# One element of the last output piece is copied by ScalarE and VectorE and multiplied by TensorE ahead of the program's final branch

## The chip, the cores and the metric

The kernel runs on one core of a Trainium2 chip. A core has five engines with instruction streams of their own: TensorE (PE; its weight loads are listed as PEld), VectorE (DVE), ScalarE (ACT), GpSimd (POOL) and SyncE (SP), which here issues the DMAs. The metric is the device time of one execution in microseconds (us); lower is better. Names that end in q in the profile (PEldq, ACTq, DVEq, SPq) stand for an engine's sequencer: the part that reads the stream, waits on semaphores, branches and issues DMAs.

## The reference, cut to what matters

```python
for t in range(S):                      # S = 768, per batch (4) and head (8), D = 48
    cur = u * k[t] ⊗ v[t]
    y[t] = r[t] @ (state + cur)
    state = w * state + k[t] ⊗ v[t]
x = y rearranged to [3072 tokens, 384]
h = x @ w_in                            # 384 x 2048
g = 0.5 * h * (1 + erf(h / sqrt(2)))
out = g @ w_out                         # 2048 x 384
```

A decaying recurrence over 768 positions comes first, then a two-layer perceptron on its 3072 rows of 384 numbers.

## The kernel before, in words

The recurrence is cut into 6 chunks of 128 positions and computed with matrix products, in 24 groups (6 chunks by 4 pairs of heads). The perceptron runs behind it, chunk by chunk: 512 rows at a time, the 2048 hidden features in 16 blocks of 128, which makes 96 steps. A step has nine products that make the hidden block (`product1`, L697, into `Hp`), a GELU on ScalarE (L729, L730), a difference on VectorE (L731) and nine products that add to the three output banks (`product2`, L741, into `O0`, `O1`, `O2`).

The order of all work is set ahead of time by the class `Plan`. Every piece of work is given to it by `add(engine, ns, due, function, r=names read, w=names written)`, or by `dma(...)` for SyncE. `Plan.run` then plays the list through with estimated times and lets each engine take the piece with the earliest due time among those that could start; the functions are called in that order, and this is the order of each engine's stream. The waits between engines are put in by the framework from the tiles that are read and written.

The last step is written out in `moe2`. Its output is cut into four pieces: two of 512 columns from banks O0 and O1, and two of 256 columns from O2 and Y. ScalarE (L780) and VectorE (L777) in turn multiply a bank by 256 into an SBUF tile (`raw0`, `raw1`, `raw2`, and for the last piece `Nb`, called `N[NP]` in the code), and SyncE stores each piece with a DMA of its own (L783). The last piece is made by VectorE.

Behind the planned work stands `with tc.If(plain[0] < LP * NP)` (L918). It holds a general version of the kernel, for decay rates that lie outside a range that is tested on the chip. Every engine compares the count that it loaded at L807 and branches. With these inputs the condition is false, and each engine jumps over the general version to the program's end (L1004), where a barrier gathers all five engines: SyncE first waits there for all DMAs to land. The general version is long on TensorE and ScalarE, short on the others.

Of the kernel before, what the change touches and what calls it, by code (L numbers as in the profile page):

```python
# [9 lines left out]
F32 = mybir.dt.float32  # L10
# [46 lines left out]
class Plan:  # L57
# [16 lines left out]
    def add(self, eng, ns, at, fn, r=(), w=(), port=False):  # L74
        n = len(self.ops)
        deps = set()
        for x in r:
            deps.add(self.writer.get(x))
            self.readers.setdefault(x, []).append(n)
        for x in w:  # L80
            deps.add(self.writer.get(x))
            deps.update(self.readers.pop(x, ()))
            self.writer[x] = n
        deps -= {None, n}
        self.ops.append((eng, ns, at, fn, deps, port or eng == "pool"))
        self.reads.append(set(r))
        self.writes.append(set(w))
        return n

    def dma(self, nbytes, at, fn, r=(), w=()):  # L90
        self.add("sp", nbytes, at, fn, r, w)
# [99 lines left out]
def rwkv_gelu_mlp(tc, rkT, rkv, wuT, uN, wmlp, r, k, vT, w, u, out):  # L191
    nc = tc.nc
    with ExitStack() as ctx:
        cst = ctx.enter_context(tc.tile_pool(name="cst", bufs=1))
# [6 lines left out]
        def sb(shape, dt, name, pool=None):  # L201
            return (pool or wk).tile(shape, dt, name=name)

        AA = psp.tile([128, 2, 512], F32, name="A")
        A = [AA[:, i] for i in range(2)]
# [47 lines left out]
        add, dma = plan.add, plan.dma  # L253
        dve = lambda n: 65 + n / 0.96
        dve2 = lambda n: 65 + n / 1.92
        act = lambda n: 60 + n / 1.2
# [30 lines left out]
        for dst, src, x in ((diag2, diag, "diag"), (past2, past, "past")):  # L287
            for h in range(2):
                add("act", 245, LATER, lambda dst=dst, src=src, h=h: nc.scalar.copy(
                    out=dst[64 * h:64 * h + 64], in_=src[64 * h:64 * h + 64, 64 - 64 * h:128 - 64 * h]),  # L290
                    r=[x], w=[f"{x}2{h}"])
# [21 lines left out]
        for x in wa:  # L313
            add("act", act(2 * DM), LATER, lambda x=x: nc.scalar.copy(
                out=x.bitcast(F32).rearrange("p (a n) -> p a n", a=2),
                in_=zeros[:, 0:DM].bitcast(F32).unsqueeze(1).to_broadcast([128, 2, DM])), r=["zeros"], w=["wa"])
# [223 lines left out]
        U0 = NB * HALF  # L540
        SLOTS = NP + 1
        done = sb([1, 1], F32, "done", cst)

        quarter = lambda x: slice(64 * x, 64 * x + D)
        heads = lambda x: slice(D * x, D * x + D)
# [154 lines left out]
        def hidden(m):  # L700

            i, k_ = NCH % 2, NSTEP - 1 - m
            if k_ == 5:
                return x3[:, 0], x3[:, 1], "x3h", "x3l"
            if k_ >= 3:
                return gh[m % 2], gl[m % 2], f"gh{m % 2}", f"gl{m % 2}"
            return xx[i][:, 0, k_], xx[i][:, 1, k_], f"xx{i}{k_}h", f"xx{i}{k_}l"
# [30 lines left out]
        def product2(j, high, low, n, part):  # L738
            wt, gt = ((wh, high), (wl, high), (wh, low))[n]
            d, dst, a, b = part  # L740
            nc.tensor.matmul(dst[:, a:b], lhsT=wt[j][:, 1, d * 128:(d + 1) * 128], rhs=pairs(gt)[:, a // 2:b // 2],  # L741
                             start=(j == 0 and n == 0), stop=(j == NJ - 1 and n == 2))

        def moe2(m, at, dest):
            t, j = divmod(m, NJ)
            parts = LAST if t == NCH - 1 else PARTS
            banks = ["O0", "O1", "O2", "Y"][:len(parts)]

            def go(m, n, which, at):
                j = m % NJ  # L750
                high, low, GH, GL = hidden(m)
                add("pe", MM * sum(parts[i][3] - parts[i][2] for i in which) / TOK, at, lambda: [product2(j, high, low, n, parts[i]) for i in which],
                    r=[f"{('wh', 'wl', 'wh')[n]}{2 * j + 1}", (GH, GH, GL)[n]], w=[banks[i] for i in which])


            if m == 0:
                for which in ((0, 1), (2,)):
                    for n in range(3):
                        go(m, n, which, at + n)
            elif m < NSTEP - 2:  # L760
                for n in range(3):
                    go(m, n, range(len(parts) if m < NSTEP - LEFT else 2), at + n + 2000 * (m == NSTEP - 3 and n == 2))
            elif m == NSTEP - 1:
                for q, i in ((1, 0), (1, 1), (5, 2), (4, 2), (0, 0), (0, 1), *((q, 2) for q in range(LEFT - 3, -1, -1)),
                             *((q, 3) for q in range(LEFT - 1, -1, -1))):
                    at += 2000
                    for n in range(3):
                        go(m - q, n, (i,), at + n)
            if j < NJ - 1:
                return  # L770
            last = m == NSTEP - 1
            for i, (d, bank, a, b) in enumerate(parts):

                o, R = (raw[i], f"raw{i}") if last and i < 3 else (N[NP], f"Nr{NP}") if last else (raw[0], "raw0")
                o = flat2(o).bitcast(F32)[:, 0 if last else d * TOK:][:, 0:b - a]
                if i % 2:
                    add("dve", 65 + (b - a) / 0.96, at + 1000 + i, lambda o=o, bank=bank, a=a, b=b: nc.vector.tensor_scalar(  # L777
                        out=o, in0=bank[:, a:b], scalar1=256.0, scalar2=None, op0=ALU.mult), r=[banks[i]], w=[f"{R}{'' if last else i}"])
                else:
                    add("act", 50 + (b - a) / 1.2, at + 1000 + i, lambda o=o, bank=bank, a=a, b=b: nc.scalar.mul(  # L780
                        out=o, in_=bank[:, a:b], mul=256.0), r=[banks[i]], w=[f"{R}{'' if last else i}"])
                if last:
                    dma(512 * (b - a), at + 2000, lambda d=d, a=a, b=b, o=o: nc.sync.dma_start(dest[d][:, a:b], o), r=[R])  # L783
            if not last:
                dma(128 * 6144, at + 20000, lambda: nc.sync.dma_start(
                    dest.rearrange("d p n -> p d n"), flat2(raw[0]).bitcast(F32).rearrange("p (d n) -> p d n", d=3)),
                    w=[f"raw0{i}" for i in range(3)])
# [77 lines left out]
        for n, x in enumerate(LOADS):  # L865
            at, behind = AT_LOADS + 1000 * n, []
# [24 lines left out]
        def step_at(m):  # L891
            return FIRST + STEP * min(m, 5 * NJ) + STEP_LAST * max(m - 5 * NJ, 0)

        for G in range(NSTEP + 1):
            if 0 <= G < NJ:
                if G >= 3:
                    w_load(G, step_at(G) - WEIGHT_AHEAD)
                w_split(G)
            if G < NSTEP:
                moe1(G, step_at(G))  # L900
            if G == 0:
                group(NP, LATER)
            if G % 4 == 0 and G // 4 + NP < NG:
                gi = G // 4 + NP + 1
                at = step_at(4 * (gi - 1 - NP)) + GROUP_DUE
                if 5 < gi < NG:
                    load_group(gi, at - GROUP_AHEAD)
                group(gi, at)
            if G >= 1:
                moe2(G - 1, step_at(G) + 2000, out[(G - 1) // NJ])  # L910
            if G == 2 * NJ:
                count_plain(step_at(G))
# [5 lines left out]
        with tc.If(plain[0] < LP * NP):  # L918
# [6 lines left out]
            with tc.For_i(0, NCH, 1) as c:  # L925
# [7 lines left out]
                o = g.tile([128, 3, TOK], F32, name="og")  # L933
# [75 lines left out]
```

## Time and profile before

| | us |
|---|---|
| median of 3 runs | 454.14 (454.06 to 455.35) |
| the profiled execution | 454.08 |
| its span, first to last instruction | 452.3 |
| TensorE busy in the span | 441.3 (98%) |
| VectorE, ScalarE, GpSimd busy | 229.3, 186.1, 69.0 |

The profiled execution is 0.06 us off the median, and 1.8 us of it lie around the span. Up to 446.7 us TensorE has next to no gap. Behind it come 5.6 us without a product: the last piece's scaling, its store, the branch and the barrier. These are too small for the costliest groups of the page; they are read from the timeline of the last microseconds, from the rows of the branch's line (L918) and of the program's end (L1004), and from the DMA view of short windows.

### The profile page before, as it was taken

The page shows a single profiled execution, that of the slowest core. Times are in us where ns is not written, and L with a number is a line of the kernel's source. Part 1 is how long each engine was busy: PE and PEld are TensorE (multiplying, and loading weights), DVE is VectorE, ACT ScalarE, POOL GpSimd, SP SyncE. Part 2 cuts the span into 40 slices and gives each one's busy share as a digit, 9 for nine tenths or more (in the row PEclk, how much of TensorE's full clock was granted, in tenths as well). Part 3 has the DMA queues.
Part 4 walks back from the last instruction along what each step waited for, and adds up shares of the span by engine and source line. Part 5 has one row for each costly group of instructions (what it writes and reads, how often), then busy time and mean ns, then how long its engine had stood idle before and what let it go on. Part 6 is the DMA issues. An engine that isn't in the chain of part 4 may idle for free.

```text
span 452.3 us, 10294 instructions
## 1 busy us (share of the span) xinstructions
PE 441.3 (98%) x4526; PEld 380.2 (84%) x4526; DVE 229.3 (51%) x343; ACT 186.1 (41%) x333; POOL 69.0 (15%) x91
## 2 busy tenths in 40 slices
PE   8999999999999999999999999999999999999995
PEld 7777878888888888888888888888888888888884
DVE  7899978875354538253554544545435311211111
ACT  9989998524222233222233222323223222322221
POOL 1351011330211221102302202112012000000000
PEclk9999999999999999999999999999999999999999
DMA  8988674334031234030332321312503000100002
GB/s 298 364 325 296 237 245 147 112 113 152 19 113 52 62 112 161 10 111 1 113 95 73 115 61 52 112 43 68 171 5 107 15 0 13 70 1 1 1 0 75
DMA packets 15426, 46.60 MB, mean 103 GB/s; under 512 B 3664, under 2 KB 4048, under 8 KB 15376
## 3 DMA queue, kind: packets, MB, share of 16 engines
q1 hardware_dynamic: 15376, 45.88, 30.5%
q8 instruction: 37, 0.61, 0.6%
q14 instruction: 13, 0.11, 0.1%
HBM read 38.73 MB, written 4.72 MB: 96 GB/s over the span
## 4 chain that ended last, share of the span: by engine, by line
PE 84%; ACT 7%; DVE 3%; DMA 3%; SPq 1%; issue 1%
PE Hp L697 38%; PE O L741 36%; PE Y L607 2%; ACT wa L396 2%; PE Y L635 2%; PE A L615 2%; ACT wh L405 1%; DMA N<-in_rkv_dram 1%; DMA E<-W 1%; PE A L624 1%; ACT wb L399 1%; PE Y L741 1%; SPq L367 1%; DVE wb L401 1%; ACT gh L729 1%
## 5 line engine op out<-in xcount | busy, mean ns | idle before, releaser
L697 PE MATMUL Hp<-xx,wh 128*128 128x512 f32 x570 | 156.6, 383 | 0.7 <-ACT gf L730 0.7
L731 DVE TENSOR_TENSOR gl<-gf,gh 128x512 fp32r<-128x512 f32 x92 | 68.8, 748 | 142.3 <-ACT gf L730 141.7
L729 ACT ACTIVATE gh<-Hp 128x512 fp32r<-128x512 f32 x91 | 54.3, 597 | 191.5 <-PE Hp L697 191.4
L697 PEld LDWEIGHTS Hp<-xx,wh 128*128 128x128 f32 x570 | 105.5, 189 | 16.8 <-ACT gf L730 1.1
L697 PE MATMUL Hp<-xx,wl 128*128 128x512 f32 x285 | 77.7, 380 | 0.0
L741 PE MATMUL O<-gh,wh 128*128 128x512 f32 (+1 forms) x276 | 74.6, 377 | 2.1 <-ACT gh L729 2.0
L741 PE MATMUL O<-gl,wh 128*128 128x512 f32 (+1 forms) x276 | 74.0, 375 | 0.0
L741 PE MATMUL O<-gh,wl 128*128 128x512 f32 (+1 forms) x276 | 73.9, 375 | 0.0
L741 PEld LDWEIGHTS O<-gh,wh 128*128 128x128 f32 x276 | 51.6, 189 | 11.7 <-ACT gh L729 4.7
L697 PEld LDWEIGHTS Hp<-xx,wl 128*128 128x128 f32 x285 | 53.6, 189 | 7.7
L741 PEld LDWEIGHTS O<-gl,wh 128*128 128x128 f32 x276 | 51.3, 189 | 7.1 <-issue 0.3
L741 PEld LDWEIGHTS O<-gh,wl 128*128 128x128 f32 x276 | 51.3, 189 | 6.8
L730 ACT ACTIVATE gf<-Hp 128x512 f32<-128x512 f32 x95 | 56.2, 592 | 0.0
L562 POOL TENSOR_TENSOR Nb<-Nb 128x384 f32<-128x384 f32 x20 | 21.1, 1053 | 131.5 <-DMA Nb<-in_rkv_dram 69.6
L559 DVE TENSOR_TENSOR Tb<-Tb,E 112x1024 f32<-112x1024 f32 x20 | 25.6, 1280 | 2.9 <-DMA Tb<-in_rkT_dram 2.8
L664 DVE SCALAR_TENSOR_TENSOR Sb<-Sa,E,A 48x192 f32<-48x192 f32 x40 | 16.5, 413 | 16.5 <-PE A L624 15.8
L565 POOL TENSOR_TENSOR Nb<-Nb,WN 128x384 f32<-128x384 f32 x20 | 20.6, 1032 | 21.5 <-DVE wl L408 13.3
L434 ACT CAST xx<-Y 112x512 fp32r<-112x512 f32 x15 | 8.8, 587 | 35.6 <-PE Y L635 35.6
L568 POOL TENSOR_TENSOR Nb<-Nb,u_sb 128x384 f32<-128x384 f32 x20 | 20.7, 1034 | 8.3 <-DVE gl L731 7.3
L571 DVE TENSOR_REDUCE cs<-Nb 128x8 f32<-128x384 f32 x20 | 11.0, 550 | 19.5 <-POOL Nb L568 19.5
L396 ACT ACTIVATE wa<-raw 128x768 f16<-128x768 bf16 x16 | 18.9, 1188 | 0.0
L645 POOL MEMSET done<- 1x1 f32 x19 | 1.7, 90 | 112.2 <-PE Y L607 112.2
(125 smaller groups left out, 387.9 us busy)
## 6 DMA issues: line engine op xcount, KB each, us to landing
raw<-in_wmlp_dram SPq DMA_DIRECT2D x16, 767.8 KB, 6.0
Nb<-in_rkv_dram SPq DMA_DIRECT2D x20, 576.0 KB, 5.5
Tb<-in_rkT_dram SPq DMA_DIRECT2D x20, 512.0 KB, 4.0
out_dram<-raw SPq DMA_DIRECT2D x5, 768.0 KB, 3.6
T<-in_rkT_dram SPq DMA_DIRECT2D x4, 512.0 KB, 5.2
xx<-x SPq DMA_DIRECT2D x30, 64.0 KB, 4.0
N<-in_rkv_dram SPq DMA_DIRECT2D x4, 384.0 KB, 7.1
out_dram<-raw SPq DMA_DIRECT2D x2, 256.0 KB, 4.7
```

The source lines that it names most:

```text
L396: add("act", 930, LATER, lambda: nc.scalar.activation(out=a.bitcast(F16).rearrange("p (n t) -> p n t", t=2)[:, :, 1], in_=top.bitcast(BF16 ...
L559: add("dve", 1140, LATER, lambda: nc.vector.tensor_tensor(out=flat, in0=flat, in1=E[:, p, 0].rearrange("l h i -> l (h i)").unsqueeze(1).to ...
L562: add("pool", pool(DM), LATER, lambda: nc.gpsimd.tensor_tensor(out=n[:, 0], in0=n[:, 0], in1=n[:, 1], op=ALU.mult), r=[NK], w=[NR])
L565: add("pool", pool(DM), LATER, lambda: nc.gpsimd.tensor_tensor(out=kn, in0=kn, in1=WN2[:, p].rearrange("s j d -> s (j d)").unsqueeze(1).to ...
L568: add("pool", pool(DM), LATER, lambda: nc.gpsimd.tensor_tensor(out=n[:, 0], in0=n[:, 0], in1=u_sb[:, p, :].unsqueeze(1).to_broadcast([C, N ...
L571: add("dve", 465, LATER, lambda: nc.vector.tensor_reduce(out=sums, in_=n[:, 0].rearrange("s b (j d) -> s (b j) d", d=D), axis=AX.X, op=ALU ...
L664: add("dve", 430, at, lambda l=l, x=x: nc.vector.scalar_tensor_tensor(out=out[quarter(1 - x)], in0=src[l], scalar=E[l, p, 1, h, 32:33], in ...
L697: nc.tensor.matmul(dst, lhsT=wt[j][:, 0, k_ * 128:(k_ + 1) * 128], rhs=pairs(x[:, a, k_, :]), start=start and k_ == ks[0], stop=stop and k ...
L729: add("act", 480, LATER, lambda: nc.scalar.activation(out=high, in_=dst, func=AF.Gelu, scale=256.0), r=[H_], w=[GH])
L730: add("act", 480, LATER, lambda: nc.scalar.activation(out=gf, in_=dst, func=AF.Gelu, scale=256.0), r=[H_], w=["gf"])
L731: add("dve", dve(512), LATER, lambda: nc.vector.tensor_tensor(out=low, in0=gf, in1=high.bitcast(F32), op=ALU.subtract), r=["gf", GH], w=[G ...
L741: nc.tensor.matmul(dst[:, a:b], lhsT=wt[j][:, 1, d * 128:(d + 1) * 128], rhs=pairs(gt)[:, a // 2:b // 2], start=(j == 0 and n == 0), stop= ...
```

## The change

A tile `held_back` of one partition and two elements is added among the constants. Where the last step's pieces are done, three more pieces of work are given to the plan. ScalarE copies element [0, 0] of the last piece into the tile's first element. VectorE copies that into the second. TensorE multiplies the second with itself into one element of bank A. Nothing reads the product.

```diff
+        held_back = sb([1, 2], F32, "held_back", cst)
...
-            if not last:
+            if last:
+                first, second = held_back[:, 0:1], held_back[:, 1:2]
+                add("act", 200, at + 3000, lambda: nc.scalar.copy(out=first, in_=o[0:1, 0:1]), r=[R], w=["first"])
+                add("dve", 100, at + 3001, lambda: nc.vector.tensor_copy(out=second, in_=first), r=["first"], w=["second"])
+                add("pe", 60, at + 3002, lambda: nc.tensor.matmul(A[0][0:1, 0:1], lhsT=second, rhs=second, start=True, stop=True),
+                    r=["second"], w=["A0"])
+            else:
```

`o` and `R` are those of the loop's last pass, the piece that VectorE made. No other row of any engine's stream is moved. The prediction speaks of the ends of two streams. ScalarE's ended so (line, operation, tiles and waits; the tiles' numbers and the waits' names are the framework's):

```order
L729 ACTIVATE xx_122<-Hp 128x512 [waits PE_49]
L730 ACTIVATE gf<-Hp 128x512 [waits DVE_49]
L780 ACTIVATE raw_130<-O_70 128x512 [waits DMAHW1_49,PE_49]
L780 ACTIVATE raw_132<-O_72 128x256 [waits PE_49]
L918 COMPARE_AND_BRANCH
```

and ends so now, one line further down in the file at the first rows and seven at the last:

```order
L731 ACTIVATE gf<-Hp 128x512 [waits DVE_49]
L781 ACTIVATE raw_130<-O_70 128x512 [waits DMAHW1_49,PE_49]
L781 ACTIVATE raw_132<-O_72 128x256 [waits PE_49]
L787 COPY held_back<-Nb_112 1x1 [waits DVE_49,Pool_49]
L925 COMPARE_AND_BRANCH
```

ScalarE's branch stood right behind its own last piece; now a copy that waits for VectorE's piece stands between. VectorE's stream has one row more in the same place, between its last piece and its branch: the copy from `first` to `second`, which waits for ScalarE. TensorE's last rows before, the end of the last piece's 18 products:

```order
L741 MATMUL Y<-xx_122,wl_457 128x256
L741 MATMUL Y<-xx_122,wh_456 128x256
L741 MATMUL Y<-xx_122,wh_458 128x256
L741 MATMUL Y<-xx_122,wl_459 128x256
L741 MATMUL Y<-xx_122,wh_458 128x256
L918 COMPARE_AND_BRANCH
```

and now:

```order
L742 MATMUL Y<-xx_122,wh_457 128x256
L742 MATMUL Y<-xx_122,wh_459 128x256
L742 MATMUL Y<-xx_122,wl_460 128x256
L742 MATMUL Y<-xx_122,wh_459 128x256
L789 MATMUL A<-held_back 1x1 [waits DVE_49]
L925 COMPARE_AND_BRANCH
```

TensorE's branch had no wait on another engine close ahead of it; now a product that waits for VectorE stands right before it. SyncE's four stores and its branch, and GpSimd's stream, read as before. In the built program the new tile takes 32 bytes of each partition, so the working tiles behind the constants (`Tb`, `Nb`, `raw`, `xx` and so on) start 32 bytes further on.

## Rows read from the trace of the kernel before

**Rows 1.** The page: span, and busy time, share, instructions of the engines.

```profile
span 452.3 us, 10294 instructions
PE 441.3 (98%) x4526; PEld 380.2 (84%) x4526; DVE 229.3 (51%) x343; ACT 186.1 (41%) x333; POOL 69.0 (15%) x91
```

**Rows 2.** Timeline, last microseconds: start, length, engine, line, operation, out<-in, count [idle<-releaser].

```profile
445.48 2.44 SPq L783 DMA_DIRECT2D out_dram<-raw  x1
446.42 0.28 PE L741 MATMUL Y<-xx,wh 128*128 128x256 f32 x1
446.73 0.42 DVE L777 TENSOR_SCALAR Nb<-Y 128x256 f32<-128x256 f32 x1 [1.88 <-PE Y L741]
448.03 0.58 SPq L783 DMA_DIRECT2D out_dram<-Nb  x1
```

**Rows 3.** Branch line L918 from 440 to 450: engine, operation, durations ns, first/last start.

```profile
L918 PEldq COMPARE_BRANCH  x1: 4518/4518/4518, 444.5 to 444.5; - x1
L918 ACTq COMPARE_BRANCH  x1: 50/50/50, 444.7 to 444.7; - x1
L918 DVEq COMPARE_BRANCH  x1: 72/72/72, 446.7 to 446.7; - x1
L918 DVEq EVENT_SEMAPHORE  x1: 21/21/21, 447.3 to 447.3; - x1
L918 ACTq EVENT_SEMAPHORE  x1: 17/17/17, 448.0 to 448.0; - x1
L918 SPq COMPARE_BRANCH  x1: 45/45/45, 448.7 to 448.7; - x1
L918 PEldq EVENT_SEMAPHORE  x1: 51/51/51, 449.1 to 449.1; - x1
```

**Rows 4.** Program's end, L918 from 450.5, then L1004 from 449 and from 451.4.

```profile
L918 SPq EVENT_SEMAPHORE  x3: 17/17/17, 450.8 to 450.9; - x3
...
L1004 PEldq DRAIN  x1: 13/13/13, 449.3 to 449.3; - x1
...
L1004 SPq DRAIN  x2: 7/7/7, 451.5 to 451.5; - x2
```

**Rows 5.** DMA views, 444.5 to 445.5, 445.5 to 446: queue, kind: packets, MB, share of 16 engines.

```profile
q1 hardware_dynamic: 13, 0.03, 6.9%
...
q1 hardware_dynamic: 89, 0.18, 99.4%
q8 instruction: 1, 0.02, 24.9%
```

**Rows 6.** DMA view of 163.1 to 163.6, and L266 of 163 to 164, all L266.

```profile
q8 instruction: 1, 0.02, 13.4%
...
L266 SPq DMA_DIRECT2D Tb<-in_rkT_dram x1: 1644/1644/1644, 163.1 to 163.1; - x1
...
L266 SPq DMA_DIRECT2D Tb<-in_rkT_dram x20: 327/334/1644, 13.9 to 338.0; - x20
```

**Rows 7.** Landing of the last piece: line L783 from 448 to 449.

```profile
DMA to landing us min/median/max: 2.7/2.7/2.7
```

**Rows 8.** ScalarE's timeline, its last two instructions.

```profile
443.95 0.60 ACT L780 ACTIVATE raw<-O 128x512 f32<-128x512 f32 x1 [1.30 <-PE O L741]
444.72 0.39 ACT L780 ACTIVATE raw<-O 128x256 f32<-128x256 f32 x1 [0.17 <-PE O L741]
```

**Rows 9.** L697 on TensorE's sequencer at 166.5 and 237, and VectorE's timeline there.

```profile
L697 PEldq EVENT_SEMAPHORE  x1: 51/51/51, 166.7 to 166.7; - x1
...
165.95 0.69 DVE L731 TENSOR_TENSOR gl<-gf,gh 128x512 fp32r<-128x512 f32 x1 [0.42 <-ACT gf L730]
...
L697 PEldq EVENT_SEMAPHORE  x1: 51/51/51, 237.6 to 237.6; - x1
...
236.86 0.69 DVE L731 TENSOR_TENSOR gl<-gf,gh 128x512 fp32r<-128x512 f32 x1 [0.28 <-ACT gf L730]
```

**Rows 10.** Small instructions, by line: L476, L806, L804; and ScalarE's gf at 442.

```profile
L476 ACT COPY cs<-Hp x4: 140/149/166, 7.5 to 14.6; 128x8 f32<-128x8 f32 x4
...
L806 DVE CAST n<-A x1: 145/145/145, 175.4 to 175.4; 1x1 int32<-1x1 f32 x1
...
L804 PE MATMUL A<-n x2: 164/164/164, 175.2 to 175.2; 112*1 112x1 f32 x2
...
442.05 0.59 ACT L730 ACTIVATE gf<-Hp 128x512 f32<-128x512 f32 x1
442.68 0.69 DVE L731 TENSOR_TENSOR xx<-gf,xx 128x512 fp32r<-128x512 f32 x1 [2.85 <-ACT gf L730]
```

**Rows 11.** The page's groups: VectorE's scaling of each loaded group.

```profile
L559 DVE TENSOR_TENSOR Tb<-Tb,E 112x1024 f32<-112x1024 f32 x20 | 25.6, 1280 | 2.9 <-DMA Tb<-in_rkT_dram 2.8
```

## The prediction

> **What bounds the kernel now.** I read the page first: TensorE is busy 98% of a span of 452.3 us [rows 1], so an edit in the middle could only pay by shortening TensorE's own stream. This one adds one small instruction to three engines, all at the end, so the question is what ends the program. The second view is the timeline of the last microseconds [rows 2]: TensorE's last product ends at 446.70, VectorE scales the last piece from 446.73 to 447.15, but its store is only issued at 448.03. SyncE was busy with the store before it: that issue ran from 445.48 for 2.44 us.
>
> The third view, the rows of the branch's line [rows 3], shows the rest. TensorE's sequencer reached the branch at 444.5, about two microseconds before its last product, and had done with it 4.52 us later, at 449.06. ScalarE branched at 444.7 and went on at 448.0, VectorE took from 446.7 to 447.3, SyncE from 448.7 to about 449.2. Then the end [rows 4]: TensorE reaches the barrier at 449.3. SyncE waits for the stores, sees the last at about 450.8, and reaches the barrier at 451.5, last of all. So **SyncE and the last store end the program**, 2.2 us behind TensorE. From 451.5 to 452.3, 0.8 us, the barrier itself runs.
>
> What makes the third issue so long? The DMA view of two short windows [rows 5]: no instruction packet in 444.5 to 445.5; one of 16 KB begins between 445.5 and 446, some 1.0 us behind TensorE's branch. It is 24.9% of 16 engines over 0.5 us, so 1.99 us. An earlier place reads alike [rows 6]: with such a packet in flight one load's issue took 1644 ns, against a median of 334 ns. There nothing else moved in that window, and the packet took 13.4% of 8 us = 1.07 us. So TensorE's jump fetches code while the first two stores are moving; the fetch is slowed from 1.07 to 1.99 us, and the third issue, and behind it the last store, are held up with it.
>
> **The change part by part.**
>
> *What it moves.* Three branches. The chain starts at 447.15, when the last piece is made. ScalarE starts 0.04 us later (the gap between a GELU's end at 442.64 and VectorE's start at 442.68 [rows 10]) and copies in 0.15 us (149 ns for 8 elements a row); VectorE again 0.04 and 0.15 (145 ns for one element). TensorE's sequencer goes on about 0.06 us behind VectorE: twice its next entry, at 166.7 and 237.6, stands right behind the end of an L731 on VectorE, at 166.64 and 237.55, whose result a product ahead of that entry in the stream waits for [rows 9]. Sum 0.44: TensorE branches at about **447.6**, 3.1 us later than before. The product itself takes 0.16 us for each of two passes [rows 10] and runs beside the branch; it costs nothing, and would cost 0.3 us if the barrier waited on it alone.
>
> *What it frees: the stores.* With no fetch in 445.5 to 447.5 I expect the third issue at 0.33 us, the median of [rows 6], instead of 2.44. SyncE is then free when the last piece is ready, and issues its store at about 447.25 instead of 448.03: 0.8 us earlier. With the landing 2.7 us after the issue as before [rows 7] the store lands at 449.95, and SyncE reaches the barrier 0.75 us behind that, at **450.7** instead of 451.5. If the issue is long for another reason, this gain is 0; if the landing is quicker too, now that fetches aren't in its way, at most another 0.9, the time by which the fetch was stretched beside the stores. Below nothing I exclude: nothing new stands ahead of SyncE's stores.
>
> *What it delays: TensorE's arrival.* It arrives at 447.6 + d + 0.24, where d is the branch's length and 0.24 lies between 449.06 and the drain at 449.3 [rows 4]. No row shows this branch in quiet. The upper end for d is the row itself, 4.52 [rows 3]. The lower end is the 1.0 us up to the fetch, plus a quiet fetch of 1.07, plus nothing: 2.1. I take the row with its fetch at the quiet length: 4.52 - (1.99 - 1.07) = 3.6, near the upper end, since it is the same engine, the same jump and the same code. Arrival at 447.6 + 3.6 + 0.24 = **451.4**.
>
> *ScalarE and VectorE.* ScalarE branches at about 447.2 as its copy starts (before, 0.0 us behind the start of its last piece at 444.72 [rows 8, 3]); with its old 3.3 us it is through at 450.5. VectorE branches at 447.4 and is through at 448.0. Both lie ahead of TensorE.
>
> *The tile.* 32 bytes move the working tiles. No row prices an address; the place where it could show is a load that is waited for, and VectorE waits 2.8 us in all for the groups' loads [rows 11]. A tenth of that, 0.3 us, either way is my bound; I take 0, since these loads are issued well ahead.
>
> *Sum.* The barrier now waits for the later of SyncE (450.7) and TensorE (451.4): 451.4 against 451.5, so -0.1 us. Against the profiled execution 454.08 - 0.1 = **454.0 us**; the median of the runs is 0.06 us above that execution, which changes nothing. The change swaps one late arrival for another of about the same time.
>
> [...]
>
> **The rivals.**
>
> *Slower: the fetch is as slow as before, now beside the last store.* The last store's packets move from about 448.2 on; the fetch would start about 1.0 us behind the branch, at 448.6, with ScalarE's in the same stretch. If d stays 4.52, TensorE arrives at 447.6 + 4.52 + 0.24 = 452.35, 0.85 us behind the old end: 454.9 us. It decides from d = 3.7 on, which puts TensorE at 451.5. For it: the slow fetch of [rows 5] ran beside such stores. Against it: there 512 KB were in flight, here 128 KB.
>
> *The branch isn't held.* The sequencer reads past the waiting product; TensorE branches at 444.5, the fetch collides as before and the last store stays where it was: 454.1 us. Against it: [rows 9].
>
> *Faster: the jump is short in quiet.* With d of 2.8 or less TensorE is there by 450.7 and the stores end the program: 451.5 - 0.8, 453.3 us; with a quicker landing and d near 2.1 it is 452.7. For it: VectorE and SyncE are through with their branches in 0.5 to 0.6 us, in busy stretches. Against it: they run a short stretch of code past, and TensorE's own row is 4.52.
>
> **How the numbers follow.** Forecast, 451.0 to 451.9 for TensorE's arrival, 453.5 to 454.5 us: 0.5. Slow fetch: 0.2, around 454.9. Not held: 0.1, around 454.1. Short jump: 0.2, 452.7 to 453.5. A measurement of this kernel tells about 0.3% from no change, 1.4 us: 452.7 to 455.5. Only the end of the short jump with a quicker landing lies below that (0.06); only a d beyond 5.1, which no row shows, lies above (0.07); so 0.87 within. The range of 8 in 10 leaves a tenth out at each side: 453.0, inside the short jump, to 455.1, a little past the slow fetch.
>
> **What would show it.** In the changed kernel's trace the third store's issue takes about 0.33 us, the last store is issued by 447.3, TensorE's branch starts at about 447.6, and its drain stands at 451.4, later than SyncE's wait for the last store. Wrong would be: a third issue still over 1 us (then the fetch isn't what held it); a branch at 444.5 (not held); a branch shorter than 2.8 us (faster) or longer than 4 us (slower); or a difference ahead of 440 us, which only the tile's 32 bytes could make.

## The result, and the profile after

The changed kernel takes **457.74 us** (median of six executions) against 454.1 us for the kernel before, run on the same chip: a ratio of **1.0075, 95% interval 1.006 to 1.009**. Five of the six executions lie at 457.29 to 458.52 with a median of 457.64; the sixth took 2611.83 us, the record does not show why, and the ratio leaves it out. It is slower by more than the 0.3% that the prediction took as the bound, and 2.6 us above the upper end of its range. The profiled execution took 457.83 us.

First the page: the span has grown by 3.8 us against [rows 1], TensorE's busy time by 1.9.

```profile
span 456.1 us, 10301 instructions
PE 443.2 (97%) x4528; PEld 381.7 (84%) x4528; DVE 228.2 (50%) x344; ACT 186.2 (41%) x334; POOL 69.9 (15%) x91
```

Next the end: the rows of the branch's line, now L925, which answer to [rows 3], and of the stores' line, now L784.

```profile
L925 ACTq COMPARE_BRANCH  x1: 50/50/50, 450.3 to 450.3; - x1
L925 DVEq COMPARE_BRANCH  x1: 72/72/72, 450.6 to 450.6; - x1
L925 PEldq COMPARE_BRANCH  x1: 4318/4318/4318, 450.8 to 450.8; - x1
L925 ACTq EVENT_SEMAPHORE  x1: 17/17/17, 453.4 to 453.4; - x1
L925 PEldq EVENT_SEMAPHORE  x1: 51/51/51, 455.1 to 455.1; - x1
...
L784 SPq DMA_DIRECT2D out_dram<-raw x3: 344/383/402, 447.7 to 448.6; - x3
L784 SPq DMA_DIRECT2D out_dram<-Nb x1: 333/333/333, 450.3 to 450.3; - x1
```

The three branches are held, and the longest issue of the first three stores is 402 ns, where it was 2.44 us [rows 2]. The program's end (now L1011), against [rows 4], and behind it, from the view of SyncE's waits (us in total, times, longest), what SyncE waits for there:

```profile
L1011 SPq EVENT_SEMAPHORE  x10: 17/28/1527, 453.3 to 456.0; - x10
L1011 PEldq DRAIN  x2: 8/10/13, 455.4 to 455.7; - x2
```

```profile
SPq L1011 <- PEq L925: 1.5, 1, 1.5
```

SyncE, which was last before, now waits 1.5 us for TensorE's branch. That is the swap the prediction spoke of. But the clock times of all these rows are some 3 us later than it said, and so is the last product: it ends at 449.78, where it ended at 446.70. TensorE lost that time long before the end. The timeline of TensorE around 20 us shows where: first the kernel before, then the one after (start, length, engine, line, operation, out<-in, count, [idle before it <-releaser]).

```profile
19.36 0.57 PE L355 MATMUL O<-ident,E 112*128 112x112 f32 x4 [0.87 <-DMA E<-W]
19.70 1.17 PE L307 MATMUL Hp<-zeros 128*128 128x512 f32 x4
20.80 1.08 PE L504 MATMUL O<-Am,N 128*48 128x128 f32 x16
```

```profile
21.02 0.98 PE L355 MATMUL O<-ident,E 112*128 112x112 f32 x4 [2.29 <-DMA E<-W]
21.68 2.06 PE L307 MATMUL Hp<-zeros 128*128 128x512 f32 x4
23.66 1.39 PE L504 MATMUL O<-Am,N 128*48 128x128 f32 x16
```

The first product that reads the tile `E` starts 1.66 us later, and it waits for the DMA that fills `E`. The products behind it also take longer: four of L307 take 2.06 us instead of 1.17. By L504, which starts 2.86 us later, most of the delay is there; it settles at 3.09 and stays so to the last product. The same place in the chain of waits (start, length), of the kernel before and of the one after:

```profile
13.24 5.98 DMA E<-W
```

```profile
13.03 7.86 DMA E<-W
```

And how long the four `E<-W` copies (L367) took from issue to landing, before and after:

```profile
DMA to landing us min/median/max: 6.0/8.7/10.6
```

```profile
DMA to landing us min/median/max: 7.9/10.3/12.0
```

The last copy of `E` lies on the chain that sets the end, before as well as after, and the change stretched it by 1.9 us. Why the products behind it are slower is seen in the view by windows of the kernel after (columns: us, then busy share and count of PE, PEld, DVE, ACT, POOL, then the granted clock, the DMA share, GB/s):

```profile
19.00:20.00 1.00, 0.00 (x0) 0.00 (x0) 1.00 (x1) 1.00 (x3) 0.00 (x0) 1.00 0.99 290
20.00:21.00 1.00, 0.00 (x0) 0.01 (x1) 1.00 (x3) 1.00 (x2) 0.00 (x0) 0.96 1.03 372
21.00:22.00 1.00, 0.98 (x5) 1.00 (x6) 1.00 (x2) 0.97 (x2) 0.00 (x0) 0.50 1.11 367
...
24.00:25.00 1.00, 1.00 (x17) 0.81 (x13) 0.00 (x0) 0.00 (x0) 0.78 (x1) 0.83 0.99 369
```

TensorE does nothing from 19 to 21 us, and behind that idle time the granted clock falls to 0.50, until some way into the window from 24, where it is 0.83 in the mean. In the kernel before it is 1.00 in all six of these windows. So of the 3.1 us, 1.66 are the later data; the other 1.4 or so, by subtraction, are put down to the clock.

The two profiled executions differ by 3.84 us in span: 3.09 ahead of the last product's end, 0.75 behind it (5.57 to 6.32). Two questions are left for the chip: what about the change makes `E` late, and what the chain at the end costs or brings by itself.

### The profile page after: what moved, and what is told of

Read it like the earlier page. It is cut to its first block, busy times and chain, and to the rows that moved or that the text cites. A ratio compares the mean times of both kernels' runs of the same rounds, so it can differ in the third digit from the quotient of the medians.

```text
span 456.1 us, 10301 instructions
## 1 busy us (share of the span) xinstructions
PE 443.2 (97%) x4528; PEld 381.7 (84%) x4528; DVE 228.2 (50%) x344; ACT 186.2 (41%) x334; POOL 69.9 (15%) x91
## 4 chain that ended last, share of the span: by engine, by line
PE 83%; ACT 7%; DVE 3%; DMA 3%; SPq 1%; issue 1%; ACTq 0%
PE Hp L698 37%; PE O L742 36%; PE Y L608 2%; ACT wa L396 2%; PE Y L636 2%; PE A L616 2%; DMA E<-W 2%; ACT wh L405 1%; PE A L625 1%; DMA N<-in_rkv_dram 1%; ACT wb L399 1%; PE Y L742 1%; SPq L367 1%; DVE wb L401 1%; ACT gh L730 1%
## 5 line engine op out<-in xcount | busy, mean ns | idle before, releaser
L563 POOL TENSOR_TENSOR Nb<-Nb 128x384 f32<-128x384 f32 x20 | 22.3, 1113 | 136.5 <-DMA Nb<-in_rkv_dram 92.4
```

Of the source, the lines that this page charges most:

```text
L563: add("pool", pool(DM), LATER, lambda: nc.gpsimd.tensor_tensor(out=n[:, 0], in0=n[:, 0], in1=n[:, 1], op=ALU.mult), r=[NK], w=[NR])
```

## The experiments

The first theory is on place: the 32 bytes that `held_back` takes move every tile behind it, `E` among them. `E`'s four copies write rows of 256 bytes. In the kernel before, `E` begins at byte 48640 of a partition, 190 times 256; in the one after, at 48672. Its rival is the chain of three instructions itself, through the order or the end. All ratios below are against the kernel before on the same chip (medians 454.1 to 454.25 us); they are estimates from all executions that are compared and need not equal the quotient of two medians. A difference whose interval holds 1 is not clear of noise. The end is the time from the last of the working products to the end of the span, worked out from the trace.

| kernel | what it has | median us | ratio (95%) | E's first product | end |
|---|---|---|---|---|---|
| before (profiled) | | 454.1 | 1 | 19.36 | 5.57 |
| after | tile and chain | 457.74 | 1.0075 (1.006 to 1.009) | 21.02 | 6.32 |
| tile_only | tile, E at +32 | 456.71 | 1.0049 (1.0031 to 1.0066) | 20.50 | 5.06 |
| in_done | chain, E unmoved | 455.22 | 1.0014 (0.9998 to 1.0031) | 19.35 | 6.18 |
| pad256 | chain, E at +256 | 455.14 | 1.0021 (1.0005 to 1.0037) | 19.38 | 6.31 |
| e_only | E alone at +32 | 457.01 | 1.006 (1.0042 to 1.0077) | 21.49 | 4.75 |
| tile64 | tile, E at +64 | 456.85 | 1.0058 (1.0042 to 1.0073) | 20.97 | 5.04 |
| rest_only | tiles behind E at +32 | 453.77 | 0.9989 (0.9977 to 1.0001) | 19.41 | 4.56 |
| aligned_only | loads' tiles aligned | 454.76 | 1.0016 (1.0003 to 1.003) | 19.99 | 5.01 |
| no_product | the copies alone | 454.4 | 1.0003 (0.9983 to 1.0024) | 20.13 | 4.67 |
| product_only | product on last piece | 455.11 | 1.0019 (0.9996 to 1.0042) | 19.96 | 5.69 |
| drain_only | TensorE drain, no product | 454.63 | 1.0021 (0.9997 to 1.0044) | 19.66 | 5.61 |
| product_third | product on third piece | 453.55 | 1.0004 (0.9974 to 1.0033) | 19.78 | 4.56 |
| aligned_third | last and aligned_only | 453.95 | 1.0003 (0.9987 to 1.002) | 19.70 | 4.59 |

### Place or chain

**tile_only** is the kernel before with the tile, and nothing that uses it.

```diff
         done = sb([1, 1], F32, "done", cst)
+        held_back = sb([1, 2], F32, "held_back", cst)
```

> The kernel before with the tile held_back alone: 32 bytes are taken, no instruction is added. Theory of the place (the move of the working tiles by 32 bytes lets the four copies into E land 1.7 us later, and TensorE, idle longer, runs the next products at a lower clock; together 3.1 us ahead of 25 us): 457.2 us, with the last product at about 449.8 and the old end of 5.6 us. Theory of the chain (the three added instructions and the later branches cost it all): 454.1 us, last product at 446.7.

**in_done** is the changed kernel with its two elements put into the 32 bytes that `done` has anyway, so that no tile moves.

```diff
-        done = sb([1, 1], F32, "done", cst)
-        held_back = sb([1, 2], F32, "held_back", cst)
+        done = sb([1, 3], F32, "done", cst)
+        held_back = done[:, 1:3]
...
-                        p = nc.gpsimd.memset(done, 0.0)
+                        p = nc.gpsimd.memset(done[:, 0:1], 0.0)
```

> The changed kernel with the two elements put into unused room behind the tile done, so that no tile moves; the three instructions stay. Theory of the place: the last product is back at 446.7, and only the end stays longer, 6.3 us against 5.6 in the two traces: 454.8 us. Theory of the chain: 457.7 us. A third, that one more instruction on each stream shifts what is fetched with what: also 457.7, with the last product at 449.8.

**pad256** is the changed kernel with a tile of 256 bytes, so that everything moves, by a multiple of 256.

```diff
-        held_back = sb([1, 2], F32, "held_back", cst)
+        held_back = sb([1, 64], F32, "held_back", cst)
```

> The changed kernel with held_back widened to 256 bytes, so that E starts at 48896, again a multiple of 256 bytes, and every working tile moves by 256. If the offset within 256 bytes (or a smaller power of two) is what counts: as with no move, 454.8 us. If any move of the tiles does it: 457.7 us.

**e_only** is the kernel before with `E` moved by 32 bytes and all tiles behind it by 256.

```diff
+        sb([1, 8], F32, "ahead")
         E = sb([LP, NP, 2, 2, HALF], F32, "E")
...
+        sb([1, 56], F32, "behind")
```

> The kernel before with 32 unused bytes ahead of E and 224 behind it: E alone starts 32 bytes past a multiple of 256, the tiles behind it lie 256 bytes further on, the tiles ahead of it as before. If the copies into E alone make the loss: 457.2 us. If it is the loads into Tb and Nb, which share the DMA engines with these copies: 454.1 us. If both add: between, near 455.5.

The unused tile costs 2.5 us by the medians (456.71 less 454.23), the move of `E` alone 2.8, and the chain without the move 1.0 in in_done and 0.9 in pad256. The chain's part is near the noise: the interval of in_done just holds 1, that of pad256 does not. TensorE's first product on `E` in the timelines of tile_only, e_only and in_done, in that order, each in a fence of its own:

```profile
20.50 0.57 PE L355 MATMUL O<-ident,E 112*128 112x112 f32 x4 [2.27 <-DMA E<-W]
```

```profile
21.49 0.57 PE L357 MATMUL O<-ident,E 112*128 112x112 f32 x4 [3.20 <-DMA E<-W]
```

```profile
19.35 0.57 PE L355 MATMUL O<-ident,E 112*128 112x112 f32 x4 [0.86 <-DMA E<-W]
```

Behind that, the granted clock is 0.50 in tile_only and 1.00 in in_done, as one row of the view by windows shows for each, in that order (the clock stands third from the end):

```profile
23.00:24.00 1.00, 1.00 (x9) 0.64 (x6) 0.00 (x0) 0.17 (x1) 0.24 (x1) 0.50 0.98 332
```

```profile
23.00:24.00 1.00, 1.00 (x33) 1.00 (x29) 1.00 (x3) 0.00 (x0) 0.94 (x1) 1.00 0.99 403
```

In the traces the late data and the fall of the clock to 0.50 come with `E` at +32: in_done and pad256 have neither (first product on `E` at 19.35 and 19.38, clock 1.00 from 19 to 27 us), though their chain is that of the changed kernel. So it is the tile that costs most, by moving `E`.

### Which move of E, and which side of the copies

**tile64** moves `E` by 64 bytes, to tell a step of 64 bytes from one of 256.

```diff
+        held_back = sb([1, 16], F32, "held_back", cst)
```

> The kernel before with an unused tile of 64 bytes among the constants: E starts 64 bytes past a multiple of 256. If a 256-byte row that crosses a multiple of 256 is what costs: as the tile of 32 bytes, 456.7 us. If it is a 64-byte grain: 454.2 us.

**rest_only** leaves `E` and moves all behind it, the tiles of the groups' loads among them, by 32.

```diff
         E = sb([LP, NP, 2, 2, HALF], F32, "E")
+        sb([1, 8], F32, "behind")
```

> The kernel before with 32 unused bytes behind E: E stays at a multiple of 256 bytes, the tiles behind it (the groups' Tb and Nb, raw, xx and so on) start 32 bytes further on, as in the changed kernel. If the place of E alone makes the body's loss, as e_only (2.8 us with E alone moved) has it: 454.2 us, as before. If the loads into Tb and Nb share in it: 455 to 456 us.

**aligned_only** leaves `E` and puts what stood beside a multiple of 256 onto one: the tiles `T` and `N` that the first loads fill, and half of the rows of `W` that the copies read.

```diff
+        sb([1, 24], F32, "behind_w", pro)
...
+        sb([1, 48], F32, "behind_all", pro)
```

> The kernel before with two unused tiles in the early pool: the first groups' T and N start at multiples of 256 bytes instead of 192 past one, and of the 256-byte rows read from W for the copies into E half start at a multiple of 256 instead of none; E and all working tiles stay. If the place of a copy's far side counts for these loads and for reads as it does for E: the copies into E land 0.5 to 1 us earlier and TensorE restarts earlier, 453.0 to 453.7 us. If only E's side counts: 454.2 us.

At +64 `E` is as late as at +32, and the clock falls as well in the trace, to 0.50. One of tile64's ten executions kept a mean clock of 1.000, and it took 454.79 us against 456.33 to 458.03 for the other nine, whose clock was 0.989 to 0.996. rest_only costs nothing. aligned_only was expected to gain and did not: its median is 0.6 us above the kernel before, and its first product on `E` came no earlier. The first products on `E` in tile64 and in rest_only:

```profile
20.97 0.87 PE L355 MATMUL O<-ident,E 112*128 112x112 f32 x4 [2.05 <-DMA E<-W]
```

```profile
19.41 0.58 PE L356 MATMUL O<-ident,E 112*128 112x112 f32 x4 [1.19 <-DMA E<-W]
```

A count from the traces goes with it. The copies of `E` are 1792 packets of 256 bytes. Their mean time is 24.4 to 25.0 ns in the four profiled kernels with `E` at +32 or +64 (after, tile_only, e_only, tile64), and 18.7 to 19.5 ns in the ten with `E` at a multiple of 256. TensorE's first product on `E` starts at 20.50 to 21.49 us in the four and at 19.35 to 20.13 in the ten. So it is the written side of these short rows that counts. Which feature of the place it is, is less sure. +32 and +64 cost and +256 does not, which fits rows that cross a multiple of 256 bytes, but no run has `E` at +128. Nor does each crossing row pay: half of the packets take 18 to 21 ns in either group, while a quarter take 29 ns or more with `E` at +32 or +64 and under a twentieth with `E` on a multiple of 256. Spread over 16 engines, the longer packets add 0.6 to 0.7 us to the time of each, between a third and a half of the 1.1 to 2.1 us by which TensorE's first product on `E` was late; the rest is not accounted for.

The runs show a cost on the written side alone: with half of the rows read from `W` put on a multiple of 256, aligned_only gained nothing (454.76 us, first product on `E` at 19.99 against 19.36). How such a row is moved, and why it takes longer, no run shows.

### What the chain at the end does

**no_product** is in_done without the product: the copies stay, TensorE is not held.

```diff
-                add("pe", 60, at + 3002, lambda: nc.tensor.matmul(A[0][0:1, 0:1], lhsT=second, rhs=second, start=True, stop=True),
-                    r=["second"], w=["A0"])
```

> No tile moves (the two elements lie behind done). ScalarE's and VectorE's copies stay, the product is left out, so TensorE branches as in the kernel before, 2.15 us ahead of its last product's end. If TensorE's late arrival is the whole cost of the chain: third store's issue long again (1.9 to 2.4 us), end of 4.8 to 5.6 us behind the last product, 454.2 us, no difference from before. If the copies and the later branches of ScalarE and VectorE cost something by themselves: 455 us.

**product_only** has no tile and no copies; the product reads the last piece itself.

```diff
+                add("pe", 60, at + 3002, lambda: nc.tensor.matmul(A[0][0:1, 0:1], lhsT=o[0:1, 0:1], rhs=o[0:1, 0:1], start=True, stop=True),
+                    r=[R], w=["A0"])
```

> No tile moves. No copies; the product takes the last piece's element itself and waits for VectorE directly, so TensorE branches about 0.5 us behind its last product instead of 1.0, while ScalarE and VectorE branch as before. TensorE's branch takes its fetch's length plus about 2.5 us in all six traces so far (2.34 to 2.58). With ScalarE's fetch out of the way the fetch is 1.1 to 1.7 us, so arrival 0.5 + 3.6 to 4.2 + 0.25 = 4.35 to 4.95, end 5.1 to 5.7 us: 454.2 to 454.6 us. If the branch's length does not depend on the fetch's neighbours: 4.2 again, 454.6 us.

**drain_only** puts a drain of TensorE in the product's place, which is meant to hold its stream until its own last product is through.

```diff
+                add("pe", 60, at + 3002, lambda: nc.tensor.drain(), w=["Y"])
```

> No tile moves. No copies and no product; TensorE's sequencer waits for its own last product (a drain) and branches at about 0.1 us behind it. The third store's issue is short, the fetch starts 1.1 us behind the last product, beside the last store. Arrival 0.1 + 3.6 to 4.2 + 0.25 = 3.95 to 4.55; the stores' side, last store issued at 0.52, is at the barrier by about 4.1. End 4.8 to 5.3 us: 453.6 to 454.1 us, if a hold of TensorE's branch frees the stores and is short enough. If a hold can't pay at all: 454.5 us or more.

**product_third** lets the product wait for ScalarE's third piece (`raw2`), so that the branch is held only until all three of the earlier stores are due.

```diff
+                add("pe", 60, at + 3002, lambda: nc.tensor.matmul(A[0][0:1, 0:1], lhsT=flat2(raw[2]).bitcast(F32)[0:1, 0:1],
+                    rhs=flat2(raw[2]).bitcast(F32)[0:1, 0:1], start=True, stop=True), r=["raw2"], w=["A0"])
```

> No tile moves. No copies; the product waits for ScalarE's third piece, so TensorE branches about 1.5 us ahead of its last product's end instead of 2.15. The fetch starts at -0.5, behind most of the first two stores' packets and behind the third store's issue. Third issue short (0.4 us), last store issued at 0.52 us, its landing about 2.3 us later, barrier at 3.6 to 4.1; TensorE there by 2.9. End 4.4 to 4.9 us: 453.2 to 453.7 us, faster than before. If the third store's packets are held up all the same by the fetch: end 5.1, 454.1 us.

**aligned_third** is product_third with the edit of aligned_only.

> The same places, and the product that waits for ScalarE's third piece, so that TensorE branches 0.6 us later than before (in its own run the end was 4.56 us against 4.67 to 5.57 with the old branch, median 453.55 us). If both gains hold and add: 452.3 to 453.0 us; if the places give nothing: 453.5 us; if neither gives anything: 454.2 us.

Without the product no difference from the kernel before is seen (1.0003), although ScalarE's and VectorE's branches are held as in the changed kernel (they start at 448.4 and 448.6, behind the last product's end at 447.8), and the end is 4.67 us against 6.18 in in_done. So by the traces the chain costs its time through TensorE; the times alone do not show it, since the intervals of the two kernels overlap. The branch in no_product, which starts 2.15 us ahead of the last product's end as before:

```profile
L923 PEldq COMPARE_BRANCH  x1: 3958/3958/3958, 445.6 to 445.6; - x1
```

product_only and drain_only hold the branch for less, to 0.51 and 0.11 us behind the last product (0.97 in the changed kernel). The third issue is short in both, 401 and 402 ns, and yet the end is no shorter than 5.6 us; both medians came out 0.5 us above the upper end of what was expected. The reason is another one than in the changed kernel. The rows of drain_only: TensorE's branch, the landing of the last store alone, and the two arrivals at the end.

```profile
L921 PEldq COMPARE_BRANCH  x1: 4182/4182/4182, 447.1 to 447.1; - x1
...
DMA to landing us min/median/max: 3.6/3.6/3.6
...
L1007 SPq DRAIN  x3: 7/7/7, 451.8 to 452.1; - x3
L1007 PEldq DRAIN  x2: 8/10/13, 451.5 to 452.2; - x2
```

Here SyncE is last again (451.8 against TensorE's 451.5), because the last store took 3.6 us to land; in product_only it took 3.7. In before it was 2.7 [rows 7]. In drain_only the fetch starts 1.13 us behind the last product, 0.6 us behind the store's issue, and runs 1.78 us, right beside that store. That the one slows the other is a reading of these times; no run separates the two transfers. The rows of product_third, in the same order, have neither wait:

```profile
L922 PEldq COMPARE_BRANCH  x1: 3858/3858/3858, 445.7 to 445.7; - x1
...
DMA to landing us min/median/max: 2.5/2.5/2.5
...
L1008 SPq DRAIN  x3: 7/7/7, 451.0 to 451.3; - x3
L1008 PEldq DRAIN  x2: 8/10/13, 449.8 to 451.4; - x2
```

There the branch comes 1.54 us ahead of the last product's end. Its fetch (1.28 us) starts at 446.78, behind the third store's issue (406 ns, through at 446.42), and ends as the last store's issue does (448.06 and 448.07). Its end of 4.56 us is the shortest of all kernels that change the end, and eight of its ten executions lie at 453.31 to 453.92 us. But two are at 457.34 and 458.72, and the interval holds 1. Those two have a mean granted clock of 0.990, the other eight 0.998 to 1.000: `E` on a multiple of 256 does not keep every execution from a lower clock and a longer time, though without a trace of those two it is not shown where they lost it. Also, the unchanged end runs 4.56 us in rest_only. So no gain over the kernel before is shown, nor one for aligned_third.

## Why the prediction was wrong

**The step that failed** is "The tile". It set the 32 bytes at 0 with a bound of 0.3 us, worked out from VectorE's waits for the groups' loads [rows 11]. Those loads were the wrong place: rest_only moved their tiles by 32 bytes and cost nothing. The place that counted was the copy of `E`, which stands in the chain of waits of the kernel before as a piece of 5.98 us, with TensorE waiting 0.87 us behind it. The reading began at the end of the program, because the edit is there, and took it from TensorE's 98% that the middle had nothing to lose. In fact 5.4 us of the span before the last product's end are without a product (446.7 less 441.3), and this wait for `E` is among them. A tile among the constants is not an edit at the end. Nor would a correct price for the late data have been enough, since nearly as much again (about 1.4 us beside 1.66) is put down to the clock. The prediction did name the sign by which this would show, "a difference ahead of 440 us, which only the tile's 32 bytes could make"; that is what came.

**A term that was mis-sized** is d, the length of TensorE's branch: 3.6 us with a quiet fetch was expected, 4.32 came. The build of the sum held, but for one trace. The length less the fetch is 2.58 us in the changed kernel (4.32 - 1.74), 2.53 in the one before (4.52 - 1.99), 2.90 in rest_only and 2.34 to 2.58 in the other eleven. What failed was the fetch's 1.07, read from a place where nothing else moved [rows 6]. The DMA view of 451 to 452 in the changed kernel shows it beside the last store's packets, at 10.9% of 16 engines over 1 us:

```profile
q1 hardware_dynamic: 136, 0.12, 34.8%
q8 instruction: 1, 0.02, 10.9%
```

That is 1.74 us. So the first rival came in, the slow fetch beside the last store, which had a chance of 0.2. It stood at d = 4.52 and 0.8 us over the kernel before; d of 4.32 and a median 1.0 us over it in in_done are near that. By itself this miss would have left the time at the upper end of the range (in_done's 455.22 against 455.1). The reason given against it, that only 128 KB are in flight there, did not carry.

Why the fetch is slow stays open, though. In rest_only, whose branch is not held, it ran beside the earlier stores and was as short as in quiet: 12.2% of 16 engines over the 0.5 us from 445.8 is 0.98 us, with the stores' packets taking 94.6%.

```profile
q1 hardware_dynamic: 99, 0.17, 94.6%
q8 instruction: 1, 0.02, 12.2%
```

So the reading of [rows 5], that stores in flight slow the fetch, does not hold each time.

**What held**, with the 3.09 us of the body taken off the rows of the changed kernel:

- TensorE's branch at 447.6: 450.75 - 3.09 = 447.66. The parts of the chain were 190 ns on ScalarE and 141 on VectorE, where 0.15 each was taken.
- The branch is held by the product that waits, so the rival "not held" falls: it starts 0.97 us behind the last working product, as the product that waits for VectorE does. product_only, drain_only and product_third say the same: the branch follows the end of what is waited for each time (0.51 and 0.11 us behind the last product, and 1.54 us ahead of its end where the third piece is waited for).
- The third issue at 0.33 us: 0.40. The last store's issue at 447.25: 447.22. Its landing in 2.7: 2.8.
- ScalarE through at 450.5, VectorE at 448.0: 450.3 and 448.1.
- SyncE at the barrier at 450.7: its 1527 ns of waiting for TensorE end at 455.3, so begin at 453.8 - 3.09 = 450.7. TensorE, at 451.4 by the prediction, came at 455.35 - 3.09 = 452.26; 0.72 of the 0.86 us is d, the rest small differences on either side of it.

**Against what the end was counted** is a smaller fault. The sum stood on the end of one profiled execution, 5.57 us. Six other profiled kernels that leave TensorE's branch as it was (tile_only, e_only, tile64, rest_only, aligned_only, no_product) have ends of 4.56 to 5.06. The fetch of that one execution was long as well (1.99 us, against 0.98 to 1.67 in those six), and its last store was issued 1.34 us behind the last product, against 0.52 to 0.98 in the six and 0.52 in the changed kernel. In rest_only the fetch started 1.49 us behind TensorE's branch, where it was 1.03 in the kernel before, and the third issue was over by then; it took 403 ns without any hold (TensorE's branch, and the three earlier stores):

```profile
L919 PEldq COMPARE_BRANCH  x1: 3878/3878/3878, 444.4 to 444.4; - x1
...
L784 SPq DMA_DIRECT2D out_dram<-raw x3: 344/383/403, 444.4 to 445.3; - x3
```

So the collision that the change was to remove is not there in every execution, the stores had less to win than the 0.8 us of the sum, and the chain cost more than the 0.75 us by which the two profiles differ: in_done's end of 6.18 lies 0.6 to 1.6 above all seven.

By the medians the parts add up: 2.5 us for the tile's move and 1.0 for the chain make 3.5, and the change cost 3.5 (457.64 less 454.1). The chain's 1.0 is the less sure of the two, as its interval says.

## What to carry to other kernels

Before a small tile is counted as free, work out which addresses it shifts, and look at the DMAs with short rows that some engine already waits for: 32 bytes in front of `E` cost 2.5 us here, and the same two elements inside a slot that was there left the copies of `E` as they were. Where a wait is put ahead of a branch, ask what will be moving when the branch fetches its code: holding it for the last piece moved the fetch from the earlier stores to the last one, and SyncE waited 1.5 us for TensorE at the end. Read the end of a program from several profiled executions before a gain of under a microsecond is worked out from it.

## What the runs showed of the hardware that was not expected

- Writes of 256-byte rows between two tiles of the same core took 18.7 to 19.5 ns a packet in the mean where the rows start at a multiple of 256 bytes (ten traces), and 24.4 to 25.0 ns where they start 32 or 64 bytes past one (four traces). Aligning half of the rows read gained nothing (aligned_only, 454.76 us), and the larger loads into tiles 32 bytes off cost nothing (rest_only, 453.77 us).
- A delay of 1.1 to 2.1 us in TensorE's data came with a further loss of about 1.4 to 1.8 us, put down to the granted clock, which fell to 0.50 behind the idle time in every profiled kernel with `E` off 256 and in none with `E` on it (tile_only: products on `E` 1.14 us later, the last product 2.73 later, so 1.6 for the clock).
- TensorE's jump over the general version took 3.7 to 4.5 us in the fourteen traces, wherever it was put, of which the code fetch is 1.0 to 2.0 us and the rest 2.3 to 2.6, or 2.9 in rest_only.
- SyncE's issue of the third store took 1.9 to 2.4 us where TensorE's fetch started about 1.0 us behind an early branch (before, tile_only, e_only, tile64, aligned_only, no_product), and 0.40 to 0.41 in the eight others.
